# Fewer first-mixture steps woven between the attention's chunks, fewer weights prepared early, and a 64-wide attention state

## The chip, the cores and the metric

The kernel runs on one core of a Trainium2 chip. The metric is the device time of one execution in microseconds (us). Five engines work side by side, each through its own instructions in a fixed order: TensorE (PE; its weight loads are listed apart as PEld), VectorE (DVE), ScalarE (ACT), GpSimd (POOL) and SyncE (SP), which here only issues DMA transfers. An engine that meets an instruction whose input is not there waits, and everything behind it on that engine waits too.

## The reference, cut to what matters

Three layers follow each other: a decayed linear attention, a first mixture layer (one dense feed-forward with weights given as float64), and a second mixture in which every token goes to one of eight experts.

```python
# attention: q, k, v are (2, 8, 768, 64); lam has one decay per head
out   = (q k^T * lam^(i-j)) v  +  (q * lam^(i+1)) state       # per chunk
state = lam^chunk * state + (k * lam^(chunk-1-i))^T v         # per head, 64 x 64
# first mixture: x is (1536, 512), w_in (512, 2048), w_out (2048, 512), float64
h = x @ w_in ; g = h * cos(h) ; x2 = g @ w_out
# second mixture: 8 experts, w1 (8, 512, 1024), w2 (8, 1024, 512)
e = argmax(x2 @ w_gate)
out = softmax_e * sigmoid_e * (relu(x2 @ w1[e]) @ w2[e])
```

## The kernel before, in words

**Attention.** The work is cut into 12 units `u` (6 chunks of 128 positions times 2 batches). A loop of rounds `i` starts unit `i` with `a_s1` (transposes of k and q, the products with decay powers), unit `i-1` with `a_s2` (scores `sc`, masked to `pt` on DVE), unit `i-2` with `a_s3` (state update `sn` and output `o`). Two heads share 128 partitions: rows 0 to 63 of a tile belong to one head, rows 64 to 127 to the other. The state `st` of a batch is kept as four 128 x 128 blocks, one for each pair of heads, in which only the two 64 x 64 blocks on the diagonal are other than zero; they are set to zero once by GpSimd, and the product of q with the state (line 382) takes a whole 128 x 128 block.

**First mixture.** Tokens are cut into 6 blocks `j` of 256, the 2048 hidden columns into 8 slices `p`. One step ("B", j, p) is 24 matmuls of 256 columns (`mm_l1`, line 444, into `h`), a chain that ACT and DVE share (`cos_chain`, lines 473 to 479, into `g`), and 12 matmuls of 512 columns (`mm_l2`, line 456, into `acc`). All operands are kept as a high and a low part, which is why a step has three products for each pair of tiles.

**Weights.** Each slice has 2 pieces of w_in and 2 of w_out, 512 KB each as float64. `w_split` turns one piece into two fp32r tiles: ACT line 205, DVE lines 206, 207 and 209, ACT line 217, GpSimd line 218; then it starts the next load. `SPLITS` says how many pieces are split in each attention round, `ready(i)` how many must be split when step `i` is written after the attention.

**The order of the steps.** `HP` is the number of slices with which blocks 0 to 2 begin while the attention still runs: `FIRST * HP` steps stand there, one a round from round `START` on. Their half sums are put aside (`half_evac`), their inputs are written to DRAM (`x_d`). Then blocks 3 to 5 go through all 8 slices, and last blocks 0 to 2, read back as `xback`, go through the slices that are left. After that come the second mixture's experts.

**Order on the engines.** Within each engine the instructions do not simply stand as the source is written: when the kernel is built, a scheduler sets their order, so a step may stand earlier than the round in which the source has it.

Of the kernel before, what the change touches and what calls it, by code (L numbers as in the profile page):

```python
# [8 lines left out]
F32 = mybir.dt.float32  # L9
F32R = mybir.dt.float32r  # L10
# [18 lines left out]
def kernel(  # L29
# [14 lines left out]
    nc = tc.nc  # L44
# [77 lines left out]

    HP = 3
    steps = [("B", j, p) for j in range(FIRST) for p in range(HP)]
    NSA = len(steps)
    steps += [("B", j, p) for p in range(NP) for j in range(FIRST, NB)]
# [3 lines left out]
    order.sort(key=lambda z: min(i for i, y in enumerate(steps) if y[2] == z[1]) + 2 * (z[0] == "out"))  # L132

    def ready(i):
        return 0 if i < NSA else 4 * HP + 2 + i - NSA


    def place(w, e, p):
# [138 lines left out]

    dec = att.tile([128, H, CH], F32, name="dec")
    lpow = att.tile([128, PR, CH], F32, name="lpow")
    st = [att.tile([128, PR, 128], F32, name=f"st{i}") for i in range(B)]  # L280
    for i in range(B):
        nc.gpsimd.memset(st[i], 0.0)
    nc.vector.memset(quarter, 0.25)
    nc.vector.memset(magic, MAGIC)
    warm = const.tile([128, 1], F32, name="warm")
# [35 lines left out]
    def xs_tile(slot, name="xs"):  # L321
        return xs_p.tile([128, 2, KD, TB], F32R, tag=f"xs{slot}", name=name)
# [42 lines left out]
    def a_s3(u):  # L365
        if u < 0:
            return
        c, b = divmod(u, B)
        vs = qkv.pop((u, "v"))
        pt = p_t.pop(u)  # L370
        if c + 1 < NCH:
            kd = kd_t.pop(u)
            sn = ps_tr.tile([128, PR, 128], F32, tag="tr", name="sn")
            for h in range(H):
                sl = slice(64 * (h % 2), 64 * (h % 2) + 64)
                nc.tensor.matmul(
                    sn[sl, h // 2, sl], lhsT=kd[:, h, :], rhs=vs[:, h, :], start=True, stop=True)
        o = ps_o.tile([128, PR, 128], F32, tag="o", name="o")
        if c > 0:
            qw = qw_t.pop(u)  # L380
            for pr in range(PR):
                nc.tensor.matmul(  # L382
                    o[:, pr, :], lhsT=st[b][:, pr, :], rhs=qw[:, pr, :],
                    start=(pr == 0), stop=False, skip_group_check=True)
        for pr in range(PR):
            for j in range(2):
                nc.tensor.matmul(  # L387
                    o[64 * j:64 * j + 64, pr, :], lhsT=vs[:, 2 * pr + j, :], rhs=pt[:, 2 * pr + j, :],
                    start=(c == 0 and pr == 0), stop=(pr == PR - 1), skip_group_check=True)
        if c + 1 < NCH:  # L390
            if c > 0:
                nc.gpsimd.tensor_mul(
                    out=st[b], in0=st[b], in1=lpow[:, :, CH - 1:CH].to_broadcast([128, PR, 128]))
            for j in range(2):
                sl = slice(64 * j, 64 * j + 64)
                if c > 0:
                    nc.vector.tensor_add(out=st[b][sl, :, sl], in0=st[b][sl, :, sl], in1=sn[sl, :, sl])
                else:
                    nc.vector.tensor_copy(out=st[b][sl, :, sl], in_=sn[sl, :, sl])
        j, cols = u // 2, slice((u % 2) * 128, (u % 2) * 128 + 128)  # L400
        if j >= FIRST:
            if u % 2 == 0:
                xt[j] = xt_p.tile([128, KD, TB], F32, tag="xt", name=f"xt{j}")
            nc.scalar.copy(out=xt[j][:, :, cols], in_=o)
            return
        if u % 2 == 0:
            xsp[j] = xs_tile(j)
        hi, lo = xsp[j][:, 0, :, cols], xsp[j][:, 1, :, cols]
        nc.scalar.copy(out=hi, in_=o)
        nc.vector.tensor_sub(out=lo, in0=o, in1=hi.bitcast(F32))  # L410
# [371 lines left out]
    def first(i):  # L782
        ph, j, p = steps[i]
        if ph == "B":
            while nxt["split"] < min(wide, ready(i)):
                late(i - 2, w_split)
            if i == NSB - FIRST * REST:
                clear_rows()
            if p == HP and j < FIRST:
                xsp[j] = xback[j]  # L790
            h = mm_l1(("in", p), xsp[j])
            g_t[i] = cos_chain(h)
            if i < NSA and p == 0:
                nc.sync.dma_start(out=x_d[j], in_=xsp[j].bitcast(F32))
            if j == (NB if p < HP else FIRST) - 1:
                del wt["in", p]
            if (j, p) == (NB - 1, HP):
                for z in range(FIRST):
                    t = wa_p.tile([128, 2, KD, TB], F32R, tag=f"w{z}", name="xback")
                    nc.sync.dma_start(out=t.bitcast(F32), in_=x_d[z])  # L800
                    xback[z] = t
        elif ph == "H":
            y_t[i] = h_l1(j[0], xsp[j], p, turn)
            if i == NSB:
                h_prep(1, 0)
            if j[1] == 1:
                del wt["w1", j[0], 2 * p], wt["w1", j[0], 2 * p + 1]
            if j == (HALVED - 1, 1) and p == 1:
                c_prep(HALVED)
        else:  # L810
            g_t[i] = relu_chain(mm_l1(("w1", j, p), xsp[j]))
            del wt["w1", j, p]
            if p == 2:
                c_prep(j + 1)
# [84 lines left out]
        if i == NSB + 2 * HALVED:  # L899
            h_prep(1, 1)  # L900

    SPLITS = [0, 2, 2, 2, 2, 2, 2]
    START = 4
    for i in range(NU + 2):
        a_load(i + 2)
        if i == 0:
# [146 lines left out]
```

## Time and profile before

| | |
|---|---|
| median of 3 runs | 572.25 us (571.47 to 573.07) |
| the profiled execution, its own time | 571.74 us |
| its span | 569.9 us |
| PE busy | 541.4 us, 95% |
| DVE, ACT, POOL busy | 60%, 54%, 18% |

The span is what the profile covers; 1.84 us of the execution's own time lie around it. Busy times are shares of the span. A row of the timeline gives its start, how long it lasted, the engine and line, the names, the number of instructions, and in brackets how long the engine stood idle ahead of it and what it waited for. The granted clock is given as a share of TensorE's full speed: 1.00 is 2.4 GHz, 0.50 is 1.2 GHz.

### The profile page before, as it was taken

How to read it: one execution, taken by the hardware profiler on the slowest of the kernel's cores; microseconds unless marked ns; L12 is line 12 of the kernel's file. 1: busy time of each engine (PE TensorE's matmuls, PEld its weight loads, DVE VectorE, ACT ScalarE, POOL GpSimd, SP SyncE). 2: the span in 40 equal slices, each digit the busy share in tenths (PEclk: the TensorE clock that was granted, in tenths of full speed). 3: DMA queues.
4: the chain of work that ended last, by engine and by line, in shares of the span. 5: the costliest groups of instructions: out<-in, count | busy, mean ns of one | idle time of the engine just before them, and what ended most of it. 6: DMA issues, size and time to landing. Idle time of an engine off the chain costs nothing.

```text
span 569.9 us, 9766 instructions
## 1 busy us (share of the span) xinstructions
PE 541.4 (95%) x3860; PEld 482.3 (85%) x3860; DVE 340.9 (60%) x614; ACT 307.1 (54%) x492; POOL 104.8 (18%) x131
## 2 busy tenths in 40 slices
PE   8678999999999999999999999989999999999993
PEld 7567878888899999998988898787989999899982
DVE  4889956466776665334557577752686675755010
ACT  3465644456776667445555559624667563644010
POOL 4444520103322213000011120021011101011011
PEclk9888999999999999999999999999999999999998
DMA  8977892011455235600127245573488887650000
GB/s 211 269 193 239 227 264 82 1 38 39 155 178 185 86 99 214 205 1 0 39 102 235 80 152 172 186 239 101 161 283 291 281 255 228 207 198 27 0 26 33
DMA packets 84295, 85.22 MB, mean 150 GB/s; under 512 B 41486, under 2 KB 66062, under 8 KB 83472
## 3 DMA queue, kind: packets, MB, share of 16 engines
q1 hardware_dynamic: 82000, 78.09, 44.6%
q0 software_dynamic: 2240, 6.42, 2.9%
q8 instruction: 32, 0.52, 0.4%
q14 instruction: 23, 0.19, 0.1%
HBM read 67.31 MB, written 18.24 MB: 150 GB/s over the span
## 4 chain that ended last, share of the span: by engine, by line
PE 44%; issue 27%; DMA 11%; DVE 9%; ACT 5%; POOL 4%; SPq 1%; POOLq 0%; DVEq 0%; ACTq 0%
PE h L444 19%; PE acc L456 17%; DMA out_dram<-y,who 4%; DMA xs_d<-xrow,si 3%; POOL out_dram L645 2%; PE sc L360 2%; DMA raw<-in_moe_w_dram 2%; PE o L382 1%; PE o L387 1%; DVE a L475 1%; DVE pt L362 1%; DVE w_w L193 1%; ACT w_w L192 1%; DVE x L207 1%; DMA rows<-xs_d 1%
## 5 line engine op out<-in xcount | busy, mean ns | idle before, releaser
L456 PE MATMUL acc<-w_out,g 128*128 128x512 f32 x576 | 142.0, 394 | 1.2 <-ACT g L478 1.1
L456 PEld LDWEIGHTS acc<-w_out,g 128*128 128x128 f32 x576 | 104.6, 188 | 22.8 <-issue 1.6
L444 PE MATMUL h<-xs,w_in 128*128 128x256 f32 x792 | 104.1, 287 | 6.5 <-DVE a L477 3.9
L444 PEld LDWEIGHTS h<-xs,w_in 128*128 128x128 f32 x792 | 99.8, 194 | 11.1 <-DVE a L477 4.6
L193 DVE TENSOR_TENSOR w_w<-raw,w_w 128x1024 fp32r<-128x1024 f32 x64 | 76.8, 1222 | 26.5 <-ACT w_w L192 26.1
L192 ACT CAST w_w<-raw 128x1024 fp32r<-128x1024 f32 x64 | 65.6, 1048 | 39.0 <-DMA raw<-in_moe_w_dram 35.2
L475 DVE SCALAR_TENSOR_TENSOR a<-a,t 128x512 f32<-128x512 f32 x48 | 35.5, 739 | 66.4 <-ACT a L474 66.3
L444 PEld LDWEIGHTS h<-xs,w_w 128*128 128x128 f32 x576 | 71.8, 191 | 2.1 <-DVE g L702 0.3
L444 PE MATMUL h<-xs,w_w 128*128 128x256 f32 x576 | 72.6, 282 | 0.0
L456 PE MATMUL acc<-w_w,g 128*128 128x512 f32 x288 | 69.9, 392 | 0.0
L456 PEld LDWEIGHTS acc<-w_w,g 128*128 128x128 f32 x288 | 52.6, 188 | 10.0
L473 ACT ACTIVATE t<-h,quarter 128x512 f32<-128x512 f32 x48 | 33.0, 688 | 48.1 <-PE h L444 46.6
L645 POOL DMA_INDIRECT out_dram<-y,who x16 | 19.3, 1205 | 161.0 <-ACT y L642 157.3
L444 PE MATMUL h<-xback,w_in 128*128 128x256 f32 x360 | 46.2, 282 | 0.0
L478 ACT CAST g<-a 128x512 fp32r<-128x512 f32 x48 | 29.7, 620 | 30.4 <-DVE a L477 30.3
L444 PEld LDWEIGHTS h<-xback,w_in 128*128 128x128 f32 x360 | 43.7, 188 | 1.1 <-issue 0.8
L477 DVE TENSOR_TENSOR a<-t,h 128x512 f32<-128x512 f32 x48 | 32.8, 683 | 16.0 <-ACT t L476 14.4
L476 ACT ACTIVATE t<-a 128x512 f32<-128x512 f32 x48 | 30.3, 632 | 20.5 <-DVE a L475 20.5
L479 DVE TENSOR_TENSOR g<-a,g 128x512 fp32r<-128x512 f32 x48 | 34.5, 719 | 11.3 <-ACT g L478 9.8
L474 ACT ACTIVATE a<-t,magic 128x512 f32<-128x512 f32 x48 | 34.8, 725 | 1.3
L218 POOL TENSOR_TENSOR w_in<-x,w_in 128x512 fp32r<-128x512 f32 x16 | 22.7, 1420 | 55.3 <-ACT w_in L217 55.3
L702 DVE SCALAR_TENSOR_TENSOR g<-h,g 128x512 fp32r<-128x512 f32 x24 | 16.5, 686 | 24.5 <-ACT g L701 24.5
(145 smaller groups left out, 631.3 us busy)
## 6 DMA issues: line engine op xcount, KB each, us to landing
raw<-in_moe_w_dram SPq DMA_DIRECT2D x64, 512.0 KB, 5.0
raw<-in_moe_w_in_dram SPq DMA_DIRECT2D x16, 512.0 KB, 4.7
raw<-in_moe_w_out_dram SPq DMA_DIRECT2D x16, 512.0 KB, 3.4
xs_d<-zrow SPq DMA_DIRECT2D x16, 266.0 KB, 4.4
x_d<-xrow SPq DMA_DIRECT2D x6, 532.0 KB, 3.1
rows<-xs_d SPq DMA_DIRECT2D x6, 532.0 KB, 3.7
k<-in_k_dram SPq DMA_DIRECT2D x12, 256.0 KB, 4.0
q<-in_q_dram SPq DMA_DIRECT2D x12, 256.0 KB, 4.6
```

Source lines behind the costliest of these rows:

```text
L192: nc.scalar.copy(out=t[:, 0, :], in_=r)
L193: nc.vector.tensor_sub(out=t[:, 1, :], in0=r, in1=t[:, 0, :].bitcast(F32))
L444: nc.tensor.matmul(h[:, f * n:(f + 1) * n], lhsT=wA(key, ws, kk, f), rhs=x[:, xx, kk, :], start=(z == 0), stop=(z == 3 * KD - 1))
L456: nc.tensor.matmul(accs[t], lhsT=g[:, gs, f, t * 128:(t + 1) * 128], rhs=wB(key, ws, f), start=(first and n == 0), stop=(last and n == 5))
L473: head = nc.scalar.activation(out=t, in_=h, func=AF.Identity, bias=quarter, scale=INV2PI / WIDE)
L474: heads.append((head.ins, nc.scalar.activation(out=a, in_=t, func=AF.Identity, bias=magic).ins))
L475: nc.vector.scalar_tensor_tensor(out=a, in0=a, scalar=MAGIC, in1=t, op0=ALU.subtract, op1=ALU.subtract)
L476: nc.scalar.activation(out=t, in_=a, func=AF.Sin, scale=-TWOPI)
L477: nc.vector.tensor_mul(out=a, in0=t, in1=h)
L478: nc.scalar.copy(out=g[:, 0].rearrange("p f t -> p (f t)"), in_=a)
L479: nc.vector.tensor_sub(out=g[:, 1].rearrange("p f t -> p (f t)"), in0=a, in1=g[:, 0].rearrange("p f t -> p (f t)").bitcast(F32))
L645: put = nc.gpsimd.indirect_dma_start(out=out, out_offset=bass.IndirectOffsetOnAxis(ap=who, axis=0), in_=y, in_offset=None, bounds_check=NT ...
```

## The change

Blocks 0 to 2 take two slices instead of three between the attention's chunks, so six steps stand there instead of nine, from round 6 instead of round 4. Eight weight pieces instead of twelve are split by the rounds of the attention, none in round 1; afterwards five are due for every four steps instead of four. One of the three `xback` tiles moves from a weight buffer to a buffer of x, and is read back later. The state is kept 64 wide, without the zero blocks: two 64 x 64 products for each pair of heads in place of one of 128 x 128, one DVE instruction over 128 partitions in place of two over 64, and a GpSimd product of half the width.

```diff
-    HP = 3
+    HP = 2
...
     def ready(i):
-        return 0 if i < NSA else 4 * HP + 2 + i - NSA
+        return 0 if i < NSA else 4 * HP + 2 + (i - NSA) * 5 // 4
...
-    st = [att.tile([128, PR, 128], F32, name=f"st{i}") for i in range(B)]
-    for i in range(B):
-        nc.gpsimd.memset(st[i], 0.0)
+    st = [att.tile([128, PR, 64], F32, name=f"st{i}") for i in range(B)]
...
             for pr in range(PR):
-                nc.tensor.matmul(
-                    o[:, pr, :], lhsT=st[b][:, pr, :], rhs=qw[:, pr, :],
-                    start=(pr == 0), stop=False, skip_group_check=True)
+                for j in range(2):
+                    sl = slice(64 * j, 64 * j + 64)
+                    nc.tensor.matmul(
+                        o[sl, pr, :], lhsT=st[b][sl, pr, :], rhs=qw[sl, pr, :],
+                        start=(pr == 0), stop=False, skip_group_check=True)
...
                 nc.gpsimd.tensor_mul(
-                    out=st[b], in0=st[b], in1=lpow[:, :, CH - 1:CH].to_broadcast([128, PR, 128]))
-            for j in range(2):
-                sl = slice(64 * j, 64 * j + 64)
-                if c > 0:
-                    nc.vector.tensor_add(out=st[b][sl, :, sl], in0=st[b][sl, :, sl], in1=sn[sl, :, sl])
-                else:
-                    nc.vector.tensor_copy(out=st[b][sl, :, sl], in_=sn[sl, :, sl])
+                    out=st[b], in0=st[b], in1=lpow[:, :, CH - 1:CH].to_broadcast([128, PR, 64]))
+                nc.vector.tensor_add(out=st[b], in0=st[b], in1=sn)
+            else:
+                nc.vector.tensor_copy(out=st[b], in_=sn)
...
-            if (j, p) == (NB - 1, HP):
-                for z in range(FIRST):
-                    t = wa_p.tile([128, 2, KD, TB], F32R, tag=f"w{z}", name="xback")
-                    nc.sync.dma_start(out=t.bitcast(F32), in_=x_d[z])
-                    xback[z] = t
+            back = {(NB - 1, HP): range(HP), (NB - 1, NP - 1): range(HP, FIRST)}
+            for z in back.get((j, p), ()):
+                t = xs_tile(1, "xback") if z >= HP else wa_p.tile([128, 2, KD, TB], F32R, tag=f"w{z}", name="xback")
+                nc.sync.dma_start(out=t.bitcast(F32), in_=x_d[z])
+                xback[z] = t
...
-    SPLITS = [0, 2, 2, 2, 2, 2, 2]
-    START = 4
+    SPLITS = [0, 0, 1, 1, 1, 1, 2, 2]
+    START = 6
```

What that does to the order on the engines is shown at three places. The first is PE's order around the first step, from the last output of unit 2 to the output of unit 3 (line numbers of the change are two to three lower: 441 is `h`, 327 the transposes, 374 `sn`, 358 `sc`). Before:

```order
L387 MATMUL o<-pt,v 64x128 x8
L444 MATMUL h<-xs,w_in_287 128x256 x18
L329 MATMUL tkT<-ident,k 128x128 x4
L444 MATMUL h<-xs,w_in_287 128x256 x6
L329 MATMUL tqT<-ident,q 128x128 x4
L376 MATMUL sn<-v,kd 64x64 x8
L360 MATMUL sc<-qT,kT 128x128 x8
L382 MATMUL o<-qw,st_175 128x128 x4
L387 MATMUL o<-pt,v 64x128 x8
```

And with the change:

```order
L387 MATMUL o<-pt,v 64x128 x8
L441 MATMUL h<-xs,w_in_344 128x256 x20
L327 MATMUL tkT<-ident,k 128x128 x4
L441 MATMUL h<-xs,w_in_344 128x256 x4
L327 MATMUL tqT<-ident,q 128x128 x4
L374 MATMUL sn<-v,kd 64x64 x8
L358 MATMUL sc<-qT,kT 128x128 x8
L382 MATMUL o<-qw,st_175 64x128
L327 MATMUL tkT<-ident,k 128x128 x4
L382 MATMUL o<-qw,st_175 64x128 x7
L387 MATMUL o<-pt,v 64x128 x3
L327 MATMUL tqT<-ident,q 128x128 x4
```

The first step stands at the same place in both, behind unit 2 and ahead of unit 3; what moved is behind it, where unit 3's output is now cut into pieces with other units' transposes between them.

The second place is DVE at unit 3: from the state of batch 1 to the low part of the first `g`. `x` are weight pieces, `pt` masked scores, `a` and `g` the chain of the first step. Before:

```order
L399 COPY st1_175<-sn_422 64x4x64
L475 SCALAR_TENSOR_TENSOR a_573<-a_573,t_572 128x512
L362 TENSOR_TENSOR pt_487<-sc_488,dec_172 128x4x128
L206 TENSOR_SCALAR x_445<-x_445 128x512
L362 TENSOR_TENSOR pt_487<-sc_489,dec_172 128x4x128
L207 SCALAR_TENSOR_TENSOR x_445<-raw_295,x_445 128x512
L206 TENSOR_SCALAR x_454<-x_454 128x512
L209 SCALAR_TENSOR_TENSOR x_445<-raw_295,x_445 128x512
L207 SCALAR_TENSOR_TENSOR x_454<-raw_304,x_454 128x512
L477 TENSOR_TENSOR a_573<-t_572,h_547 128x512
L209 SCALAR_TENSOR_TENSOR x_454<-raw_304,x_454 128x512
L410 TENSOR_TENSOR xs_525<-o_629,xs_525 128x4x128
```

With the change, from the same copy on:

```order
L396 COPY st1_175<-sn_391 128x256
L341 TENSOR_TENSOR qw_374<-tqT_367,lpow_173 128x512
L472 SCALAR_TENSOR_TENSOR a_688<-a_688,t_687 128x512
L360 TENSOR_TENSOR pt_445<-sc_446,dec_172 128x4x128
L360 TENSOR_TENSOR pt_445<-sc_447,dec_172 128x4x128
L474 TENSOR_TENSOR a_688<-t_687,h_662 128x512
L476 TENSOR_TENSOR g_689<-a_688,g_689 128x512
L341 TENSOR_TENSOR qw_441<-tqT_434,lpow_173 128x512
L394 TENSOR_TENSOR st0_174<-st0_174,sn_458 128x256
L360 TENSOR_TENSOR pt_523<-sc_524,dec_172 128x4x128
L360 TENSOR_TENSOR pt_523<-sc_525,dec_172 128x4x128
L407 TENSOR_TENSOR xs_486<-o_545,xs_486 128x4x128
```

The six instructions on weight pieces are gone from between unit 3's masked scores and the chain.

The third place is PE at units 4 and 5. Before (444 is the second step's `h`, 456 its predecessor's `acc`):

```order
L360 MATMUL sc<-qT,kT 128x128 x8
L444 MATMUL h<-xs,w_in_366 128x256 x18
L382 MATMUL o<-qw,st_174 128x128 x4
L329 MATMUL tkT<-ident,k 128x128 x4
L387 MATMUL o<-pt,v 64x128 x8
L456 MATMUL acc<-w_out_528,g 128x512
L329 MATMUL tqT<-ident,q 128x128 x4
```

With the change:

```order
L358 MATMUL sc<-qT,kT 128x128 x8
L387 MATMUL o<-pt,v 64x128 x3
L441 MATMUL h<-xs,w_in_489 128x256 x11
L327 MATMUL tkT<-ident,k 128x128 x4
L382 MATMUL o<-qw,st_174 64x128 x8
L387 MATMUL o<-pt,v 64x128
L327 MATMUL tqT<-ident,q 128x128 x4
L374 MATMUL sn<-v,kd 64x64 x8
L387 MATMUL o<-pt,v 64x128 x4
L358 MATMUL sc<-qT,kT 128x128 x8
L387 MATMUL o<-pt,v 64x128 x3
```

Fewer matmuls of the mixture stand between two units, and the small products of the attention follow each other in more and shorter pieces.

## Rows read from the trace of the kernel before

**Rows 1.** The page's head and its first part, PE's line.
```profile
span 569.9 us, 9766 instructions
...
PE 541.4 (95%) x3860; PEld 482.3 (85%) x3860; DVE 340.9 (60%) x614; ACT 307.1 (54%) x492; POOL 104.8 (18%) x131
```

**Rows 2.** Busy time by stretch; the columns are named in the first row.
```profile
core 0: us, PE busy (x) PEld busy (x) DVE busy (x) ACT busy (x) POOL busy (x), PEclk, DMA share, GB/s
16.00:28.00 12.00, 7.20 (x67) 5.97 (x64) 9.80 (x16) 4.63 (x8) 5.81 (x4) 0.88 0.99 263
28.00:34.00 6.00, 5.53 (x49) 4.92 (x48) 3.75 (x7) 4.08 (x7) 2.86 (x3) 0.67 1.01 283
34.00:52.00 18.00, 13.28 (x140) 10.79 (x138) 17.76 (x27) 10.03 (x18) 9.42 (x8) 1.00 0.62 165
52.00:56.00 4.00, 4.00 (x29) 3.69 (x28) 3.91 (x7) 2.08 (x4) 1.84 (x2) 0.57 0.92 324
56.00:127.00 71.00, 69.65 (x648) 60.17 (x646) 46.48 (x75) 35.72 (x58) 14.80 (x12) 1.00 0.46 127
127.00:230.00 103.00, 101.90 (x660) 92.83 (x657) 69.17 (x110) 70.71 (x112) 27.57 (x22) 1.00 0.41 140
```

**Rows 3.** PE's timeline, 16 to 28 us: three of its waits.
```profile
19.66 1.16 PE L382 MATMUL o<-qw,st 128*128 128x128 f32 x8 [1.63 <-DVE xs L410]
...
23.90 1.99 PE L444 MATMUL h<-xs,w_in 128*128 128x256 f32 x12 [1.62 <-POOL w_in L218]
26.91 1.23 PE L444 MATMUL h<-xs,w_in 128*128 128x256 f32 x4 [1.01 <-POOL w_in L218]
```

**Rows 4.** GpSimd's timeline, 20 to 24 us.
```profile
20.90 1.27 POOL L392 TENSOR_TENSOR st<-st,lpow 128x512 f32<-128x512 f32 x1 [9.02 <-PE o L382]
22.14 1.71 POOL L218 TENSOR_TENSOR w_in<-x,w_in 128x512 fp32r<-128x512 f32 x1
```

**Rows 5.** PE's timeline, 33 to 52 us: four of its waits.
```profile
33.70 1.16 PE L382 MATMUL o<-qw,st 128*128 128x128 f32 x8 [0.47 <-DVE st L399]
...
36.93 1.09 PE L387 MATMUL o<-pt,v 128*64 128x128 f32 x14 [1.35 <-DVE pt L362]
...
39.93 0.50 PE L444 MATMUL h<-xs,w_in 128*128 128x256 f32 x2 [1.33 <-DVE a L477]
...
51.65 0.51 PE L444 MATMUL h<-xs,w_in 128*128 128x256 f32 x2 [1.44 <-DVE a L477]
```

**Rows 6.** DVE's timeline, 34 to 44 us.
```profile
35.01 1.26 DVE L206 TENSOR_SCALAR x<-x 128x512 int32<-128x512 int32 x1
36.19 0.68 DVE L362 TENSOR_TENSOR pt<-sc,dec 128x512 f32<-128x512 f32 x1
...
39.20 0.67 DVE L477 TENSOR_TENSOR a<-t,h 128x512 f32<-128x512 f32 x1
```

**Rows 7.** PE's timeline, 45 to 68 us: products of the attention in unbroken runs.
```profile
45.67 1.05 PE L382 MATMUL o<-qw,st 128*128 128x128 f32 x8
46.56 0.60 PE L329 MATMUL tkT<-ident,k 128*128 128x128 f32 x4
47.09 1.09 PE L387 MATMUL o<-pt,v 128*64 128x128 f32 x16
...
61.48 1.16 PE L360 MATMUL sc<-qT,kT 64*128 64x128 f32 x16
62.57 1.16 PE L382 MATMUL o<-qw,st 128*128 128x128 f32 x8
63.66 1.09 PE L387 MATMUL o<-pt,v 128*64 128x128 f32 x16
64.68 3.01 PE L444 MATMUL h<-xs,w_in 128*128 128x256 f32 x24
```

**Rows 8.** Groups of DVE's instructions, 10 to 127 us: the state's update.
```profile
L397 DVE TENSOR_TENSOR st<-st,sn 64x256 f32<-64x256 f32 x16 | 6.7, 417 | 6.9 <-PE sn L376 4.6 <-POOL st L392 2.1
```

**Rows 9.** PE's timeline, 355 to 380 us: one wait for the chain.
```profile
362.71 3.02 PE L456 MATMUL acc<-w_out,g 128*128 128x512 f32 x12 [1.11 <-ACT g L478]
```

More of the change, by code (lines that the diff above doesn't have):

```diff
@@ L372, in a_s3 @@
             kd = kd_t.pop(u)
-            sn = ps_tr.tile([128, PR, 128], F32, tag="tr", name="sn")
+            sn = ps_tr.tile([128, PR, 64], F32, tag="tr", name="sn")
             for h in range(H):
@@ L376, in a_s3 @@
                 nc.tensor.matmul(
-                    sn[sl, h // 2, sl], lhsT=kd[:, h, :], rhs=vs[:, h, :], start=True, stop=True)
+                    sn[sl, h // 2, :], lhsT=kd[:, h, :], rhs=vs[:, h, :], start=True, stop=True)
         o = ps_o.tile([128, PR, 128], F32, tag="o", name="o")
```

## Prediction

> **What bounds the kernel now.** I read the page first. PE is busy for 541.4 of 569.9 us [rows 1], so at most 28.5 us are to be had from work that stays the same, and a part of these lies ahead of the first matmul and behind the last. The next view is the busy time by stretch [rows 2]. It shows where PE stands idle while work is left: 4.80 us from 16 to 28 us, 0.47 to 34, 4.72 to 52, nothing to 56, 1.35 to 127, and 1.10 from there to 230. So 10.0 of the 11.3 us between 16 and 127 us lie ahead of 52 us. The same rows show the granted clock: 0.88, 0.67 and 0.57 in three stretches. In clock this loses 12 x 0.12 + 6 x 0.33 = 3.4 us up to 34 us, and 4 x 0.43 = 1.7 us from 52 to 56. In both places PE had waited shortly before the clock fell [rows 3, 5].
>
> The third view is PE's timeline with its waits. From 16 to 28 us PE waits for o's single buffer (its reader on DVE, 1.63 us) and twice for the first weight tile (1.62 and 1.01 us, GpSimd line 218) [rows 3]. From 34 to 52 us it waits for DVE: for masked scores (1.35) and twice for line 477, which frees h's buffer (1.33 and 1.44) [rows 5]. DVE is busy for 17.76 of these 18 us [rows 2], and its timeline shows with what: a shift on a weight piece stands between the two halves of the masked scores and takes 1.26 us there, and more piece work stands ahead of line 477 [rows 6]. So ahead of 52 us the early weights delay the chain. Behind 56 us PE itself is the bound.
>
> **The change part by part.** Three steps leave the attention's part and come back later. A step's matmuls cost PE the same in either place, so this moves time and gains none by itself. What counts is idle time, clock and what the small products cost.
>
> *The first stretch, 16 to 28 us.* The first step stands behind unit 2 in either order, so "two rounds later" does not move it, and its two waits for weights stay. GpSimd's product of the state stands ahead of the first weight tile there, 1.27 us [rows 4]. At half the width I put it at 0.6, which brings the tile and with it the first wait 0.6 us forward (1.62 to about 1.0). The second wait hangs on the same chain and keeps its 1.0; o's buffer is freed by the same instructions as before. Idle 4.8 becomes 4.2: **-0.6**.
>
> *28 to 52 us.* The six DVE instructions on pieces between unit 3's scores and the chain are gone, so the waits there (with the smaller ones 4.72 + 0.47 = 5.19 us) [rows 2, 5] lose their cause. I lay the new order out with the durations of before. After unit 1's sn, DVE has the state (one instruction over 256 columns, 0.42 [rows 8], in place of two), qw, line 475 and two halves of pt at about 0.65 each, so about 3.0 us to the second half; PE has sc (1.09), the product with the state (0.9 to 1.1) and a transpose (0.53) [rows 7], 2.5 to 2.7. It waits about 0.5. The copy of k and q of units 3, 4 and 5 on ACT stands behind other work (a weight cast, g's cast, w_out's cast); from the same durations I get waits of 0.3, 0.45 and 0.3 at sc. Together 1.6 in place of 5.2: **-3.6**.
>
> *Clock.* The fall at 52 us came after waits that go, so I take its 1.7 us as gained. The fall ahead of 28 us came after waits of which 4.2 of 4.8 us stay, so I keep it. **-1.7**. Bounds: nothing gained, or both, -5.1.
>
> *Behind 52 us.* With fewer mixture matmuls between units, PE has less to do while a copy or a mask is made. o's buffer is freed by DVE behind two halves of pt; PE has about 2.1 us of other work there and DVE about 2.5. I put 0.2 to 0.5 us on two or three rounds: 1.35 becomes 2.0, **+0.7**. If every unit from 5 on waited 0.7 us, it would be +5.
>
> *The state's product.* Before, eight instructions for a unit take 0.89 us when a transpose of the same tile shape follows (45.67 to 46.56) and 1.09 when products of 64 columns follow (62.57 to 63.66) [rows 7]. Afterwards there are sixteen, on 64 x 64 quarters. The nearest rows are sc, sixteen instructions with half the rows in 1.09 us, and pt, sixteen with half the columns in 1.02 us [rows 7]: halves side by side share the time. Taken so, a unit's product costs what it did: 0. The trace has no product on a quarter, so the other bound is that they don't overlap: sixteen at 0.89 / 8 = 0.111 us are 1.78 us, +0.89 for each of ten units, +8.9. I take 0, because both nearest rows show the overlap. The Trainium skill (TensorEngine Tiling (Array Packing), Gotcha 1: PSUM Pressure) speaks against it: different row tiles cannot access the same PSUM bank at once. Both quarters write into the one tile o here, while sc, the only product with row halves in this trace, writes its halves into two tiles. By that rule the sum would take +8.9 in place of 0; no row shows the case.
>
> *Changes of shape.* The two times of the state's product, 1.09 and 0.89, differ by 0.20 us where the next product has another shape; other pairs give less, so I take 0.15. Counting neighbouring products of unlike shape in PE's order from the first transposes to the first full-size L2 behind the attention gives 64 before and 75 now: 11 more, **+1.6**. The same page (Key Properties) says that a change of tiling mode drains the engine; the 0.20 us agree in kind.
>
> *Weights afterwards.* 22 pieces are now split behind the attention instead of 18, five in four steps. From 127 to 230 us, with 18 of the 32 pieces, DVE is busy for 69 and ACT for 71 of 103 us [rows 2]; even if all of that were pieces, four more would add 4/18, 15 to 16 us, and leave both below 87. That is covered by PE's matmuls as long as g comes in time; a g is needed more than a whole L1 and L2 after its h. The price if the cover fails is a wait like the one of 1.11 us [rows 9], a few times. I take 0. The moved xback is read at least a dozen steps before its use: 0. Less DMA early: none of these waits of PE is for a transfer [rows 3, 5], so 0. The zeroing of the state on GpSimd lies beside the opening matmuls: 0.
>
> Sum: -0.6 - 3.6 - 1.7 + 0.7 + 1.6 = -3.6 us. Against the profiled execution's own 571.74 us that is 568.1; the median of the runs is 0.5 above that execution, so I say **568.5**.
>
> **The rivals.**
> *The quarters do not overlap* (slower). Place: line 382, ten units. Price +8.9 as above: 568.5 + 8.9 = 577. For it: both quarters end in one tile, which no pair of row halves in this trace does. (That page's rule, where it holds for quarters, gives this result.) Against it: pt's column halves also end in one tile, and overlap. From 0.36 us a unit on it eats the gain, so it decides from about 1.25 us for sixteen on. Chance 0.15.
> *The waits only change their names.* The engine orders are cut finer, and PE stops for qT, pt or o's buffer as often as before; idle from 28 to 127 us stays at 6.5 (of which I had 3.6), or the splits at five in four steps hold g up. With the 1.6 of shapes, 568.5 + 2.9 = 571.4, to 573 if the second fall of the clock stays as well. For it: less filler. Against it: DVE is relieved just where it is full. Chance 0.20.
> *The early fall of the clock goes too.* Then 3 us more, 565.5. For it: 0.6 us less idle ahead of it. Against it: 4.2 us stay. Chance 0.15.
>
> **How the numbers follow.** The forecast (565 to 570.3 by its own unknowns) has 0.50. Within 0.3% is about 1.7 us, what a measurement of this kernel can tell from no change: 570.5 to 574. Faster is the forecast and the third rival, 0.65; the same is most of the second, 0.17; slower the first and what is left, 0.18. For 8 in 10 the range reaches from 563.5, past the third rival, to 574.5, past the second; the rest is mainly the first.
>
> **What would show it.** In the changed profile: (1) the waits for line 477 and pt between 30 and 52 us are gone, DVE is clearly below 17.8 of 18 us there; (2) the first step still waits for line 218 near 23 us, by about 1.0 and 1.0 us; (3) the clock falls once, near 25 us, and not near 52; (4) sixteen products with the state take 0.9 to 1.1 us, not 1.8; (5) idle between 56 us and the attention's end is about 2 us; (6) from there on the idle time is that of before. Point 4 at 1.8, or idle behind 52 us above 5 us, would make it wrong; a clock at full from 16 us on would make it too small.

## The result and the profile after

The changed kernel takes 566.93 us (median of 5 runs, 565.06 to 567.33), the kernel before 572.25 us beside it (5 runs, 570.8 to 573.07). The ratio is 0.99, with a 95% interval of 0.9874 to 0.9926: faster by 5.3 us. The profiled execution of the changed kernel took 567.14 us, its span is 565.3 us, 4.6 below that of before [rows 1]. Line numbers after the change are 2 or 3 lower: 441 is `h`, 453 `acc`, 382 the product with the state, 470 to 476 the chain, 513 the sum of the two halves in `xrow`, 532 its transposes `x2ps`.

The page's head and PE's line, after the change:

```profile
span 565.3 us, 9913 instructions
...
PE 540.6 (96%) x3940; PEld 480.1 (85%) x3940; DVE 338.2 (60%) x604; ACT 305.3 (54%) x492; POOL 100.3 (18%) x129
```

Busy time by stretch after the change; the three steps less move the attention's end from about 139 to about 116 us, so the last two stretches begin 15 us earlier than those of [rows 2]:

```profile
16.00:28.00 12.00, 7.38 (x86) 6.16 (x86) 9.79 (x17) 5.47 (x10) 5.17 (x4) 1.00 0.92 216
28.00:34.00 6.00, 5.02 (x65) 4.19 (x64) 5.56 (x7) 3.37 (x7) 4.00 (x4) 1.00 1.04 286
34.00:52.00 18.00, 17.65 (x222) 14.18 (x219) 13.28 (x24) 8.47 (x15) 7.51 (x9) 1.00 0.96 246
52.00:56.00 4.00, 4.00 (x44) 3.03 (x44) 3.87 (x7) 3.44 (x7) 0.69 (x1) 1.00 1.07 366
56.00:112.00 56.00, 56.00 (x550) 47.49 (x550) 34.62 (x52) 28.36 (x47) 11.09 (x10) 1.00 0.36 104
112.00:215.00 103.00, 101.90 (x664) 93.18 (x663) 78.99 (x120) 73.49 (x121) 29.58 (x24) 1.00 0.50 163
```

Idle time of PE is now 4.62 us up to 28 us, 0.98 to 34, 0.35 to 52 and nothing up to 112, where [rows 2] had 4.80, 0.47, 4.72 and 1.35. DVE has 4.5 us less to do from 34 to 52 us, and the granted clock is full in every stretch.

PE's timeline after the change, 17 to 116 us: all its waits above 0.1 us, and one product with the state between rows of other products:

```profile
17.48 1.09 PE L387 MATMUL o<-pt,v 128*64 128x128 f32 x16 [0.31 <-DVE xs L407]
20.34 1.09 PE L382 MATMUL o<-qw,st 64*64 64x128 f32 x16 [1.76 <-DVE xs L407]
...
24.15 1.73 PE L441 MATMUL h<-xs,w_in 128*128 128x256 f32 x12 [1.26 <-POOL w_in L218]
27.17 0.97 PE L441 MATMUL h<-xs,w_in 128*128 128x256 f32 x6 [1.29 <-POOL w_in L218]
...
30.32 1.16 PE L358 MATMUL sc<-qT,kT 64*128 64x128 f32 x16 [0.20 <-ACT qT L329]
32.26 0.43 PE L382 MATMUL o<-qw,st 64*64 64x128 f32 x2 [0.78 <-DVE qw L341]
...
34.48 0.43 PE L387 MATMUL o<-pt,v 128*64 128x128 f32 x2 [0.18 <-DVE pt L360]
35.07 0.44 PE L387 MATMUL o<-pt,v 128*64 128x128 f32 x4 [0.17 <-DVE pt L360]
...
66.58 1.09 PE L382 MATMUL o<-qw,st 64*64 64x128 f32 x16
67.59 1.09 PE L387 MATMUL o<-pt,v 128*64 128x128 f32 x16
...
115.78 3.01 PE L441 MATMUL h<-xs,w_in 128*128 128x256 f32 x24 [1.10 <-DVE a L474]
```

The waits of [rows 5] for line 477 and for masked scores are gone or below 0.2 us; those of [rows 3] for the first weight tile have stayed. Sixteen quarter products take 1.01 us, from 66.58 to 67.59.

Far behind the attention there are new waits. PE's timeline after the change, 327 to 358 us:

```profile
327.15 0.66 PE L532 MATMUL x2ps<-ident,xrow 128*128 128x128 f32 x4 [1.02 <-DVE xrow L513]
...
329.37 0.66 PE L532 MATMUL x2ps<-ident,xrow 128*128 128x128 f32 x4 [0.97 <-DVE xrow L513]
...
357.63 3.45 PE L453 MATMUL acc<-w_out,g 128*128 128x512 f32 x12 [1.36 <-ACT g L475]
```

The last of them, for `g`, is not all new: it was 1.11 us before [rows 9]. To see where the time went I follow four places that both traces have:

| place on PE | before, us | after, us |
|---|---|---|
| scores `sc` of unit 3, behind the first step | 32.07 | 30.32 |
| third `h` behind the attention (the 1.10 wait for line 477 or 474) | 139.55 | 115.78 |
| first `x2ps` | 262.89 | 239.25 |
| first `hh`, the second mixture | 365.56 | 360.92 |
| end of the span | 569.9 | 565.3 |

A step takes 5.6 us where nothing is waited for (from 303.26 to 308.82 us in the trace of after, for one), so three steps are 16.8 us. They leave the stretch from `sc` to the third `h` and come back between `x2ps` and `hh`. Up to `sc` the change saves 1.75 us. From `sc` to the third `h` the change saves 107.48 - 85.46 - 16.8 = 5.2 us; from there to the first `x2ps` nothing (123.34 and 123.47); from `x2ps` to `hh` it loses 121.67 - 102.67 - 16.8 = 2.2 us; from `hh` on nothing (204.3 and 204.4).

### The profile page after: what moved, and what is told of

Read it like the earlier page. It is cut to its first block, busy times and chain, and to the rows that moved or that the text cites. A ratio compares the mean times of both kernels' runs of the same rounds, so it can differ in the third digit from the quotient of the medians.

```text
span 565.3 us, 9913 instructions
## 1 busy us (share of the span) xinstructions
PE 540.6 (96%) x3940; PEld 480.1 (85%) x3940; DVE 338.2 (60%) x604; ACT 305.3 (54%) x492; POOL 100.3 (18%) x129
## 4 chain that ended last, share of the span: by engine, by line
PE 51%; issue 27%; DMA 9%; DVE 4%; ACT 4%; POOL 4%; POOLq 0%; DVEq 0%; SPq 0%; ACTq 0%
PE h L441 18%; PE acc L453 18%; DMA out_dram<-y,who 4%; DMA raw<-in_moe_w_dram 3%; POOL out_dram L642 2%; PE o L387 2%; PE sc L358 2%; PE acc L730 2%; PE o L382 2%; PE hh L709 2%; DMA xs_d<-xrow,si 2%; DVE w_w L193 1%; ACT w_w L192 1%; PE sn L374 1%; PE up L266 1%
## 5 line engine op out<-in xcount | busy, mean ns | idle before, releaser
L441 PE MATMUL h<-xs,w_in 128*128 128x256 f32 x720 | 93.1, 284 | 3.7 <-POOL w_in L218 2.6
L441 PEld LDWEIGHTS h<-xs,w_in 128*128 128x128 f32 x720 | 89.4, 190 | 7.4 <-POOL w_in L218 3.0
L441 PE MATMUL h<-xback,w_in 128*128 128x256 f32 x432 | 55.5, 283 | 0.0
L441 PEld LDWEIGHTS h<-xback,w_in 128*128 128x128 f32 x432 | 52.7, 189 | 1.7 <-issue 1.2
L596 POOL DMA_INDIRECT xs_d<-xrow,si x12 | 13.6, 1136 | 105.3 <-DVE si L594 76.2
```

The costliest lines, as they stand in the source:

```text
L441: nc.tensor.matmul(h[:, f * n:(f + 1) * n], lhsT=wA(key, ws, kk, f), rhs=x[:, xx, kk, :], start=(z == 0), stop=(z == 3 * KD - 1))
```

## The experiments

All are timed against the kernel before.

**One part of the change alone.** The state alone is 64 wide, all else as before:

```diff
-    st = [att.tile([128, PR, 128], F32, name=f"st{i}") for i in range(B)]
+    st = [att.tile([128, PR, 64], F32, name=f"st{i}") for i in range(B)]
...
-                nc.tensor.matmul(
-                    o[:, pr, :], lhsT=st[b][:, pr, :], rhs=qw[:, pr, :],
+                for j in range(2):
...
+                        o[sl, pr, :], lhsT=st[b][sl, pr, :], rhs=qw[sl, pr, :],
```

> The kernel before with nothing but the 64-wide state. My theory (the state's width is worth next to nothing, the early weights are what costs): DVE stays above 9 tenths busy from 34 to 52 us, PE still waits over 3 us between 28 and 52 us, the sixteen quarter products take 1.0 to 1.1 us a unit, and the time is 571 to 573 us, within 1.5 us of before. Rival (the state's narrower GpSimd and DVE work is what gives the gain): 567 to 569 us, with the waits of 28 to 52 us gone.

Measured: 575.31 us, ratio 1.0054 (1.0034 to 1.0074). The rival that gives the state the gain falls. The loss was more than expected, and not at the quarters: sixteen of them took 1.02 us. In its trace the third `h` comes at 138.67 us, 0.9 earlier than before, and the time from there to the end is 434.8 in place of 430.35 us. The state is not used there. The trace tells where the 4.5 us lie: 1.8 between the first `x2ps` and the first `hh` (104.43 in place of 102.67 us, with a wait of 0.88 us for line 474), and 2.7 behind it, where PE's timeline has this wait (1.71 us before):

```profile
379.87 0.18 PE L580 MATMUL rps<-ohb,upper 128*128 128x8 bf16 x1 [2.77 <-DVE ohb L569]
```

The granted clock is 0.78 from 378 to 384 us there, where the kernel before has 1.00. Why DVE is later with `ohb` in this kernel no run here takes apart.

**The change without the state's part** (128 wide, as before):

> The changed kernel with the 128-wide state of before. My theory: within 1.5 us of the changed kernel, 566 to 568.5 us; the first weight wait longer by 0.3 us. Rival (the state gives the gain): 570 us and more.

Measured: 567.11 us, ratio 0.9891 (0.9865 to 0.9917): the same as the whole change. With six steps and late weights the state's part neither gives nor costs.

**The change with its weights made early:**

```diff
-    SPLITS = [0, 0, 1, 1, 1, 1, 2, 2]
+    SPLITS = [0, 2, 2, 2, 2]
```

> The changed kernel with its eight weight pieces split two a round in rounds 1 to 4 instead of one a round from round 2 on; six steps from round 6 as before. My theory: piece work stands between the masked scores again, so idle between 28 and 52 us comes back to 3 us or more, and a second fall of the clock may come back: 569 to 571.5 us. Rival (the gain is from fewer steps in the attention, whatever the weights do): 566 to 568 us.

Measured: 573.22 us, ratio 1.0005 (0.998 to 1.0031). The whole gain is lost, more than either theory's figure. Busy time by stretch and PE's waits in this kernel:

```profile
16.00:28.00 12.00, 8.72 (x79) 7.37 (x76) 9.64 (x15) 5.31 (x10) 5.55 (x5) 0.72 0.96 265
28.00:34.00 6.00, 4.38 (x61) 3.64 (x60) 4.64 (x8) 2.70 (x5) 2.06 (x3) 1.00 0.87 234
34.00:52.00 18.00, 14.69 (x146) 12.19 (x146) 15.60 (x23) 9.16 (x16) 8.57 (x8) 0.81 0.76 192
```

```profile
20.82 0.58 PE L441 MATMUL h<-xs,w_in 128*128 128x256 f32 x1 [2.97 <-ACT w_in L217]
...
31.70 1.16 PE L358 MATMUL sc<-qT,kT 64*128 64x128 f32 x16 [1.62 <-ACT qT L329]
...
38.13 0.69 PE L374 MATMUL sn<-v,kd 128*64 128x64 f32 x16 [1.42 <-ACT kT L329]
...
40.70 1.65 PE L358 MATMUL sc<-qT,kT 64*128 64x128 f32 x12 [1.89 <-ACT qT L329]
```

Idle time from 34 to 52 us is 3.31 us again, the second fall of the clock is back (0.81), and the third `h` stands at 121.78 us, 6.0 later than in the changed kernel. PE waits for ACT's copies of q and k. ACT's timeline of this kernel shows what they stand behind:

```profile
30.54 0.62 ACT L217 CAST w_in<-x 128x512 fp32r<-128x512 f32 x1 [2.18 <-DVE x L209]
31.06 0.58 ACT L329 COPY qT<-tqT 128x512 f32<-128x512 f32 x1
...
39.55 0.62 ACT L217 CAST w_out<-x 128x512 fp32r<-128x512 f32 x1 [1.47 <-DVE x L209]
40.07 0.58 ACT L329 COPY qT<-tqT 128x512 f32<-128x512 f32 x1
```

A cast of a weight piece waits 2.18 and 1.47 us for DVE's part of the split, and the copy behind it waits as long.

The waits are the smaller part of the loss. From the product `o<-pt` just ahead of [rows 3] (16.76 us here, 17.48 in the changed kernel) to the third `h`, 6.7 us are lost: PE is idle for 8.99 in place of 6.75 us, and busy for 96.03 in place of 91.55 us with as many products, under the lower clock. And the edit did more than to move the splits: the first product of the first step now stands ahead of unit 2's product with the state and waits 2.97 us for its weights (the row at 20.82 us), ahead of the clock of 0.72. In the kernels before and after it stands behind that product.

**Only the six steps** (weights early, wide state, first step in round 4):

> The kernel before with six instead of nine steps between the chunks and nothing else of the change that could matter: weights made early (0, 2, 2, 2, 2), the first step begun in round 4, the 128-wide state; the two saved blocks that come back late follow from six steps. Theory: with the wide state TensorE's order up to 34 us is that of the kernel before, so the opening costs the same as in it; what fewer steps give is the idle time of the last chunks, 2 to 3 us as between three_late and the changed kernel (569.99 and 566.93): 568.5 to 571. Rival: early weights cost the same 6 us as in early_weights whatever the state (573.2 there): 572 or more.

Measured: 572.87 us, ratio 0.9998 (0.9977 to 1.002). The rival's figure: six steps alone give nothing. PE's order at the first step is that of the kernel before, without the wait of 2.97 us. The trace has the third `h` at 118.24 us, 2.4 later than with late weights and the same state (115.81); the profiled execution, at 570.72 us, was 2.2 us faster than the median, so the trace doesn't place the rest of the 5.8 us between the two medians.

**Nine steps with late weights** and the narrow state:

```diff
-    HP = 2
+    HP = 3
...
-    SPLITS = [0, 0, 1, 1, 1, 1, 2, 2]
-    START = 6
+    SPLITS = [0, 0, 1, 1, 2, 2, 2, 2, 2]
+    START = 5
```

> The changed kernel with nine steps between the chunks again, as before, begun in round 5 (one later than before, one earlier than changed: nine do not fit behind round 6), and with the weights made late as in the change, four more of them (0, 0, 1, 1, 2, 2, 2, 2, 2). Theory: the gain comes from late weights, which leave ScalarE, VectorE and GpSimd free for the units of the first rounds; the number of steps costs nothing by itself, since a step is 5.6 us of products wherever it stands: 565 to 568.5, with waits of 3 us or less between 28 and 52 us. Rival: with nine steps the four additional splits fall into rounds in which VectorE is already full, and waits for the cosine chain and the pt products come back: 569 to 572.5.

Measured: 569.99 us, ratio 0.9954 (0.9932 to 0.9976); inside the rival's range. In its trace the third `h` comes at 134.96 us, 2.4 later than 115.78 + 16.8. So with late weights the three steps do cost 3.1 us between the chunks, most of it ahead of the third `h`. The medians side by side (the kernels differ in small things, as told above):

| steps | weights | state | us |
|---|---|---|---|
| nine | early | wide | 572.25 |
| nine | early | 64 | 575.31 |
| nine | late | 64 | 569.99 |
| six | early | wide | 572.87 |
| six | early | 64 | 573.22 |
| six | late | wide | 567.11 |
| six | late | 64 | 566.93 |

Late weights give 5.3, 5.8 and 6.3 us in their three pairs; up to the third `h` the traces show 3.7, 2.4 and 6.0 of it. In the two pairs with the narrow state, early weights come with the wait of 2.97 us at the first step (it stands at 20.88 us with the state alone, too); the pair with the wide state is free of it. Six steps give 3.1 with late weights and 2.1 or nothing with early ones. The state gives nothing with six steps, and costs 3.1 with nine and early weights.

**The start in round 4** (`START = 4`) and **one piece a step** afterwards (without `* 5 // 4`), each with all else as changed:

> The changed kernel with its first step begun in round 4, as before, instead of round 6; weights, steps and state as changed. Theory: the start in the program's order decides little, because the first step's products wait for their weights, which are made in the same places: 566 to 569. Rival: the two rounds matter, since TensorE issues in order and a step that stands ahead of the units' products holds them back while its weights are made: 569.5 to 573, with waits for line 218 of 3 us or more together and a lower granted clock between 16 and 28 us.

> The changed kernel with the later weights of the first mixture made one a step, as before, instead of five in four steps. Theory: this part of the change costs and gives nothing, since 123.3 to 123.5 us pass between the same two places (the third first half behind the attention, the first x2ps) with either rule: 566 to 568. Rival: with one a step the weights of the late part come too late for six steps, since the last products of blocks 0 to 2 need them: 569 or more, with waits for lines 217 and 218 behind 110 us.

Measured: 567.9 us, ratio 0.9899 (0.9861 to 0.9938), and 566.25 us, ratio 0.9889 (0.9861 to 0.9918). Both theories hold: these two edits do nothing that can be measured.

**The quarters in another order.** The loops over pairs and halves change places, so that four products on one quarter of the array follow each other, then four on the other:

```diff
-            for pr in range(PR):
-                for j in range(2):
+            for j in range(2):
+                for pr in range(PR):
```

> The changed kernel with the two loops around the state's product exchanged: four products on one quarter of the array, then four on the other, in the same engine order otherwise. If quarters overlap only where neighbours lie on different quarters, as my 0 for the product assumes, the sixteen instructions take about 1.7 instead of 1.0 us for a unit, and the time goes up by 5 to 8 us, to 572 to 575. If they overlap in any order, or if what bounds them is something else than the streaming, nothing changes: 566 to 568 us.

Measured: 570.99 us, ratio 0.997 (0.9947 to 0.9993), 4.1 us more than the changed kernel: less than the 5 to 8 expected, more than nothing. PE's timeline of this kernel, in which each product of the program stands as two:

```profile
68.69 1.58 PE L382 MATMUL o<-qw,st 64*64 64x128 f32 x16
70.20 1.09 PE L387 MATMUL o<-pt,v 128*64 128x128 f32 x16
```

From 68.69 to 70.20 the same sixteen products take 1.51 us in place of 1.01; ten units make 5 us, and the third `h` comes 4.7 us later (120.50). The overlap needs neighbours on different quarters; in groups of four most of it is lost (8 products of before in 0.89 us [rows 7], as sixteen without overlap, would be 1.78).

**What is lost behind the attention.** In the trace of after, the second mixture's first scales (`row_scale`, Exps on ACT and small operations on DVE, lines 613 to 632) stand among the last chains. My first theory put the 2.2 us on the Exps. Their ACT part is issued behind the last chain, in the changed kernel and in the kernel before:

```diff
-                s, who = row_scale(rows.pop(j), e, 1)
+                box = []
+                with tc.issue_after(tails[-1]):
+                    box.append(row_scale(rows.pop(j), e, 1))
+                s, who = box[0]
```

> The changed kernel, with the Exp work on the second mixture's first rows (row_scale in the steps of kind H) issued behind the last cosine chain instead of between the last chains; nothing is left out. Theory: the 2.2 to 2.4 us that the last first-mixture steps cost beyond their products come from these Exps standing between the Sin of the cosine chains on ScalarE (three extra table loads of 1.28 us and a wait for the rows' DMA), which makes x2ps wait 1.02 and 0.97 us for xrow. Then both waits go and the time falls by about 2 us against the changed kernel, to 564.5 to 565.5. Rival 1: the steps' waits only move (VectorE's chain for r_arg and r_rank or the next casts end last instead): 566 to 568, the same as the changed kernel, with new waits of the same sum on TensorE between 315 and 375 us. Rival 2: the scales are now late for the second mixture's first outputs: 568 or more.

> The kernel before with the same edit as in the run beside it: the Exp work on the second mixture's first rows behind the last cosine chain. Theory: in the kernel before this work falls where no product waits for it, so the edit gives at most the table loads' share of an already covered engine: 571.5 to 573. Rival: the same gain of about 2 us is to be had here, 569.5 to 571; then the Exps are a cost of both kernels and not what the change lost behind the attention.

Measured: 563.64 us, ratio 0.9832 (0.9799 to 0.9866), and 568.69 us, ratio 0.9933 (0.9909 to 0.9957): 3.3 and 3.5 us less than without the edit, and in both kernels more than the theory and its rival gave it. The gain is real, but the kernel before has it as well, so the Exps are not what the change lost. Nor is all of it at the place of the edit: from the first `x2ps` to the first `hh` the traces have 1.6 and 1.5 us less (120.03 and 101.14 us). The third `h`, where nothing was edited and PE's order is the same, comes 1.0 and 2.2 us earlier in these two traces. They also show what the change did lose. DVE's timeline of the changed kernel, and then of the one with late Exps:

```profile
323.62 0.15 DVE L618 TENSOR_SCALAR ng<-hrows 128x1 f32<-128x1 f32 x1 [2.33 <-DMA hrows<-xs_d]
...
325.81 0.69 DVE L474 TENSOR_TENSOR a<-t,h 128x512 f32<-128x512 f32 x1 [1.17 <-ACT t L473]
326.41 0.68 DVE L513 SCALAR_TENSOR_TENSOR xrow<-acc,part 128x512 f32<-128x512 f32 x1
...
328.63 0.68 DVE L513 SCALAR_TENSOR_TENSOR xrow<-acc,part 128x512 f32<-128x512 f32 x1
```

```profile
323.42 0.15 DVE L618 TENSOR_SCALAR ng<-hrows 128x1 f32<-128x1 f32 x1 [2.59 <-DMA hrows<-xs_d]
...
324.29 0.68 DVE L474 TENSOR_TENSOR a<-t,h 128x512 f32<-128x512 f32 x1
...
326.27 0.69 DVE L513 SCALAR_TENSOR_TENSOR xrow<-acc,part 128x512 f32<-128x512 f32 x1
```

In both, a change of sign of 0.15 us on `hrows` (the expectations call it a subtraction) holds DVE for 2.3 to 2.6 us until its DMA lands, and the chain and the `xrow` sums, for which PE waits, are queued behind it. In the kernel with late Exps PE still waited 1.35 and 0.58 us for `xrow`. In the kernel before, the change of sign stands behind the `xrow` sums; DVE's timeline there:

```profile
340.43 0.69 DVE L516 SCALAR_TENSOR_TENSOR xrow<-acc,part 128x512 f32<-128x512 f32 x1
...
341.70 0.15 DVE L621 TENSOR_SCALAR ng<-hrows 128x1 f32<-128x1 f32 x1 [0.45 <-DMA hrows<-xs_d]
```

So the second theory is this wait. Its test issues DVE's part behind the last chain too, again in both kernels:

```diff
-                with tc.issue_after(tails[-1]):
+                with tc.issue_after(tails[-2]), tc.issue_after(tails[-1]):
```

> The changed kernel with all of the second mixture's first scales (their Exps and VectorE's small operations on hrows) issued behind the last cosine chain, where the run scale_late moved the Exps alone; nothing is left out. Theory: in scale_late VectorE still stood 2.59 us before a subtraction on hrows, waiting for its DMA, with line 474 and both xrow sums queued behind it, and TensorE still waited 1.35 and 0.58 us for xrow. With VectorE free the two waits fall to 0.7 us together or less (what the sum of a finished accumulator takes), and the time falls by 1.2 to 2 us against scale_late, to 561.5 to 562.5. Rival: the waits for xrow are the order's (x2ps stands directly behind the block's last second half), so they stay at about 1.9 us, and the time stays at 563 to 564.5.

> The kernel before with the same edit. In it VectorE waited only 0.45 and 0.20 us for hrows, behind the xrow sums and not ahead of them. Theory: no further gain against the run before_scale_late: 568 to 569.5; the distance between the changed kernel and before, both with the edit, is then 6 to 7.5 us, more than the 5.3 us without it, and by so much the wait for hrows was a cost that the change's order brought. Rival: the same further gain of over 1 us, 567 or less; then the wait is no part of what the change lost.

Measured: 561.57 us, ratio 0.9818 (0.9788 to 0.9847), 2.1 us below late Exps alone, and 568.89 us, ratio 0.9956 (0.9927 to 0.9985), nothing further. The distance between the two kernels is 7.3 us. DVE's and PE's timelines of the faster one:

```profile
320.98 0.69 DVE L474 TENSOR_TENSOR a<-t,h 128x512 f32<-128x512 f32 x1
...
323.99 0.69 DVE L513 SCALAR_TENSOR_TENSOR xrow<-acc,part 128x512 f32<-128x512 f32 x1 [0.94 <-PE acc L453]
```

```profile
325.09 0.60 PE L532 MATMUL x2ps<-ident,xrow 128*128 128x128 f32 x4
...
327.07 0.66 PE L532 MATMUL x2ps<-ident,xrow 128*128 128x128 f32 x4
```

DVE does line 474 3.3 us earlier than with late Exps alone, and at `xrow` it waits for PE, not PE for it. From the first `x2ps` to the first `hh` the two kernels with this edit take 117.89 and 100.94 us, 0.15 us apart beyond the three steps, where it was 2.2. The loss is shown to be DVE's part of the scales between the last chains; the wait for the DMA, 2.3 to 2.6 us, is nearly all of that part's time. It belongs to the six steps: with these alone (weights early, state wide), PE's timeline has it too:

```profile
331.28 0.66 PE L535 MATMUL x2ps<-ident,xrow 128*128 128x128 f32 x4 [1.00 <-DVE xrow L516]
...
333.50 0.66 PE L535 MATMUL x2ps<-ident,xrow 128*128 128x128 f32 x4 [0.97 <-DVE xrow L516]
```

## Why the prediction was right, and where its terms were off

The direction and its main reason held. The range held the time; the forecast of 568.5 us was 1.6 us too high.

| term | predicted | measured, us |
|---|---|---|
| 16 to 28 us | -0.6 | -0.6 |
| 28 to 52 us | -3.6 | -3.9 |
| clock | -1.7 | -3.4 |
| idle behind 52 us | +0.7 | -1.35 |
| state's product | 0 | 0 |
| changes of shape | +1.6 | +1.7, a remainder |
| late part | 0 | +2.2 |
| PE's opening (below) | | +0.55 |

The measured terms make -4.8, the span fell by 4.6. The predicted ones made -3.6: three were off by about 2 us, two of them to the good and one to the bad.

*16 to 28 us.* The size held by luck; the way did not hold. GpSimd's product of the state took 0.90 us and not 0.6, and the waits for the first tile were 1.26 and 1.29 us where I had 1.0 and 1.0; idle time fell by 0.2 us only. I measure the term from the product `o<-pt` just ahead of [rows 3], at 16.93 us before and 17.48 after, to `sc` of unit 3. PE's timeline before, with the third `h`:

```profile
16.93 1.09 PE L387 MATMUL o<-pt,v 128*64 128x128 f32 x16 [0.53 <-DVE xs L410]
...
32.07 1.16 PE L360 MATMUL sc<-qT,kT 64*128 64x128 f32 x16
...
139.55 3.01 PE L444 MATMUL h<-xs,w_in 128*128 128x256 f32 x24 [1.10 <-DVE a L477]
```

And in the kernel before with late rows, which has before's order there and a full clock:

```profile
16.65 1.09 PE L387 MATMUL o<-pt,v 128*64 128x128 f32 x16 [0.53 <-DVE xs L410]
...
30.06 1.16 PE L360 MATMUL sc<-qT,kT 64*128 64x128 f32 x16 [0.51 <-ACT qT L331]
```

These are 15.14 us before, 12.84 after and 13.41 with the full clock. So 0.6 is the change and 1.7 the clock. Of the 0.6 us, 0.36 is the shorter wait for the first tile (1.62 us with the full clock as well), and 0.3 the shorter wait for `qT` (0.51 and 0.20 us), which I had not counted. The second wait for the tile is 1.30 us with the full clock: the 1.01 of [rows 3] was so short because PE was slow ahead of it (12 products in 1.99 us, where the full clock has 1.71). The opening is the time up to `o<-pt`; with the order of the changed kernel it varies from 16.42 us (all scales late) to 17.48, so I don't put its 0.55 us down to the change.

*28 to 52 us.* Right in place, cause and size: 5.19 us of idle time became 1.33, and putting the weights back early brought the waits, under other names, and the clock's second fall with them.

*Clock.* The step that failed is "the fall ahead of 28 us came after waits of which 4.2 of 4.8 us stay, so I keep it". 4.6 us stayed, and the changed kernel's profile has no fall. But it is not the change that decides it: the kernel before has a full clock up to 34 us in the profiles of its two late-scale runs, with the same order of PE. And the same stretch shows 0.86 in the two kernels with one piece a step and with the wide state, which are as fast as the changed one. Busy time by stretch in the former, whose order is that of the changed kernel there:

```profile
16.00:28.00 12.00, 8.63 (x84) 7.16 (x83) 9.20 (x16) 5.32 (x10) 4.80 (x4) 0.86 0.92 231
```

The third `h` comes at 115.81 us in both, against 115.78 with a full clock. PE is slower there and idle for less (3.37 us against 4.62), since the waits for weights end when GpSimd ends them. From `o<-pt` to `sc` it takes 13.11 us (17.28 to 30.39) against 12.84: this early fall, over by 28 us, cost 0.3 of the 12 x 0.14 = 1.7 us of the rows' sum. That of before reached to 34 us (0.67 [rows 2]) and cost 1.7, of 3.4 in the rows' sum. The third rival came in by name, and with it about half its price. The second fall does follow the change: from 34 to 56 us the clock is full in all eight traces with late weights, and 0.84 to 0.94 in all six with early ones.

The medians hold less of this term than the two profiles. The mean granted clock differs between executions of one kernel: in the rounds of the experiments the kernel before ran 85 times, 35 of them at 0.990 or more (571.57 us at the median) and 27 at 0.986 or less (573.43), as in its profile (0.986). The five executions of the changed kernel had 0.991 to 0.995. Against the 35, the change gives about 4.6 of its 5.3 us.

*Behind 52 us.* Predicted 0.2 to 0.5 us of wait on two or three rounds; there is none up to 112 us. The products left between the units cover every copy and mask.

*State's product.* 1.01 to 1.02 us for sixteen, as taken. By the rule of the Trainium skill (TensorEngine Tiling (Array Packing), Gotcha 1: PSUM Pressure), that different row tiles cannot access one PSUM bank at once, these products would not overlap; here they do, into one tile `o`, as long as neighbours lie on different quarters. Grouped by quarter they cost 1.51 us.

*Changes of shape.* From `sc` to the third `h`, 3.9 + 1.35 + 1.7 (second fall of the clock [rows 2]) = 6.95 us should have come; 5.2 did. The 1.7 between them is where this term lies. No run isolates it. The kernel with the wide state comes nearest: counted in its trace as in the prediction, it has 67 changes in place of 75, and takes 84.81 us from `sc` to the third `h`, 0.65 less than the changed kernel; but its product with the state differs as well.

*Late part.* "Idle as before" was wrong by 2.2 us. I had looked at whether the splits are ready in time; the new order put an instruction that waits for a DMA ahead of sums that PE needs.

The first rival (quarters) fell, though the grouped order shows how near it stood. The second (waits change their names) fell in the chunks and came true behind them, in part. What stays open is why the narrow state costs 3.1 us with nine early steps: its trace has the loss behind the attention, in a longer wait for `ohb` and a fall of the clock, and no run here took it apart.

## What to carry to other kernels

Preparatory work on the engines that feed TensorE belongs behind the stretch in which these engines are full, even if it makes nothing shorter: making the weight pieces one a round and later, not two a round from the second, gave 5 to 6 us at the median, in part through the clock, and everything else in the change little or nothing without it. An edit meant to move only the splits also moved a matmul: look at the order on the engines again before its time is read. When instructions are set in a new order, look for small ones that wait for a DMA and now stand ahead of work that the bounding engine needs, hundreds of us from the edit; here one of 0.15 us, which waited 2.3 us, took back 2 us. The changed kernel with these scales issued behind the last chain, 561.57 us, beats both kernels.

## What the runs showed of the hardware

Two 64 x 64 products on diagonal quarters of the array that end in one tile overlap when they alternate (sixteen in 1.01 us) and only in part when grouped by fours (1.51 us). A granted clock of 0.86 over 12 us cost 0.3 us where TensorE waited for weights anyway. Exps that stand between the Sins of the chains bring table loads on ScalarE, 1.28 us each; its timeline in the changed kernel:

```profile
323.84 1.28 ACT L473 ACT_TABLE_LOAD   x1
325.14 0.63 ACT L473 ACTIVATE t<-a 128x512 f32<-128x512 f32 x1
325.79 1.28 ACT L621 ACT_TABLE_LOAD   x1
```

With the Exps behind the chains, ACT has four instructions fewer (488 against 492), all of them table loads. Both kernels took 3.3 to 3.5 us less, 1.6 and 1.5 of it at this place.
